# Uniform dummy matmuls, a moved output tile and a re-fitted step order in a one-core attention-then-experts kernel

## The chip, the cores and the metric

The kernel runs on one core of a Trainium2 chip. The metric is the device time of one execution in microseconds (us); lower is better. Five engines work side by side, each through its own instructions in program order: PE (matrix products, with its weight loads listed as PEld), DVE (elementwise work and reductions), ACT (activations and copies), POOL (elementwise work, masks) and SP (which issues the transfers). They wait for each other through semaphores.

## The reference

Two stages follow each other. The first is causal attention with a bias, for 8 batches of 8 heads, 576 tokens and 64 columns per head; the second is a mixture of 4 causal attention experts on the result, of which each token uses its best 2:

```python
scores = scale * np.matmul(q, k.transpose(0, 1, 3, 2))
cum = np.cumsum(np.maximum(s, 0.0), axis=-1)
bias = -(cum[:, :, :, None] - cum[:, :, None, :])
scores = np.where(causal, -1000000000.0, scores + np.minimum(bias, 0.0))
attn = softmax(scores)                       # minus the row's maximum, sum + 1e-9
x = (attn @ v), heads side by side           # 8 x 576 x 512
logits = x @ w_gate                          # the best 2 of 4 experts, their softmax weights w
for e in range(4):
    a = softmax(causal(scale * (x @ wq[e]) @ (x @ wk[e]).T))
    out += w_e * (a @ (x @ wv[e]) @ wo[e])   # 0 for tokens that did not choose e
```

## The kernel before

The work is cut into pairs: a pair is two heads (or two experts) of one batch, and there are 50 slots for them, in the order four attention pairs of a batch and then two expert pairs of the batch before. For each pair the program has some 70 small steps, each a Python function that issues a few instructions. A step is written as slot:name, and the table STEPS lists all 3508 of them in the order in which they are issued. Nothing else sets the order: every engine takes its own instructions in that order, and SP's queue of transfers likewise. The names that matter here:

- m0 to m5 (PE, L626) form rows of bf16 scores, from which M0 to M5 (DVE, L640) take the row maxima into the tile mcol. mt (PE, L660) transposes mcol, mA (ACT) copies it as mr, and mq (SP) sends it into row 96 of the query operand. The maxima of a pair are taken one or two slots before its scores.
- h, l, lq and lk split queries and keys into a high and a low half (ACT, DVE, transfers). s0 to s6 (PE, L687 and L692) are the scores from those halves, E0 to E6 (ACT) their exponentials, d0 to d3 (POOL) the masks and the sums over keys, v0 to v7 (PE, L844) the product with the values, V0 and V1 (ACT) its copy.
- a0 and a1 (PE, L894) form the sums of two pairs; r0 (SP, L922) spreads them over partitions, r1 (DVE) takes 1/x, r2 (SP, L931) writes that to DRAM, r3 and r4 (SP, L936) read it back as rows, the tile rb. n, N and o (DVE, ACT, DVE L969) scale the values with rb and split them into xh and xl.
- p (PE, L1078) are the projections of a finished batch, P (ACT) their copies, S or the last slot's z (SP) the stores; q00 to q51 (PE, L1048) and Q0 to Q5 (ACT) are the last batch's output. Of its parts, 3 and 5 are the two 256-column halves of token tile 3, and part 4 is the tile of the last 64 tokens of two batches, whose store is two transfers.
- The bank tiles in PSUM, eight of them, are taken and given back in turn, also in the order of STEPS.

Dummies are matmuls whose result is not used. The program starts with 32 of them (FIRST_IDLE), each 128 columns long with the 64-column tile of ones as weights. 48 more (IDLE) are the steps z0 to z47 of slot -2, which STEPS spreads over the first six slots: 64 columns long, with the ones as weights if the number is even and the 128-column identity if it is odd. All of them are in float32, and the trace shows two records for one.

Of the kernel before, what the change touches and what calls it, by code (L numbers as in the profile page):

```python
# [17 lines left out]
P = 128  # L18
S = 576
HS = S // 2  # L20
D = 64
# [59 lines left out]
def heads(t, at, c0, c1):  # L81
# [252 lines left out]
def tile_attention_then_moe(ctx, tc, qk, vm, vt, s, wqk, wvg, wo, out):  # L334
# [997 lines left out]
    for k in range(FIRST_IDLE):  # L1332
        idle(0, 128)
# [9 lines left out]
    def slot(n):  # L1343
# [37 lines left out]
        if n == -2 and IDLE:  # L1381
            for k in range(IDLE):
                steps[f"z{k}"] = lambda k=k: idle(k)
# [54 lines left out]
```

## Time and profile before

| | |
|---|---|
| median of 3 timed runs | 651.64 us (648.58, 651.64, 659.48) |
| the profiled execution | 647.8 us |
| its span, first to last instruction | 646.1 us |
| PE busy | 638.1 us, 99% |
| DVE, ACT, POOL busy | 548.6, 449.2, 432.1 us |
| last matmul starts | 641.40 us |

The profiled execution's own time is 1.7 us more than its span, and below all three timed runs. A matmul's end is modelled in the trace and overlaps the next one, so PE reads as busy for as long as something follows; what counts is the distance between starts. An idle time is shown in brackets, with what ended it.

### The profile page before, as it was taken

How to read it: one execution, taken by the hardware profiler on the slowest of the kernel's cores; microseconds unless marked ns; L12 is line 12 of the kernel's file. 1: busy time of each engine (PE TensorE's matmuls, PEld its weight loads, DVE VectorE, ACT ScalarE, POOL GpSimd, SP SyncE). 2: the span in 40 equal slices, each digit the busy share in tenths (PEclk: the TensorE clock that was granted, in tenths of full speed). 3: DMA queues.
4: the chain of work that ended last, by engine and by line, in shares of the span. 5: the costliest groups of instructions: out<-in, count | busy, mean ns of one | idle time of the engine just before them, and what ended most of it. 6: DMA issues, size and time to landing. Idle time of an engine off the chain costs nothing.

```text
span 646.1 us, 16548 instructions
## 1 busy us (share of the span) xinstructions
PE 638.1 (99%) x5990; PEld 542.6 (84%) x5990; DVE 548.6 (85%) x1440; ACT 449.2 (70%) x981; POOL 432.1 (67%) x530
## 2 busy tenths in 40 slices
PE   9999999999999999999999999999999999999997
PEld 8878898878888897888888888878987889789875
DVE  8989979898888977997898879898788978873984
ACT  6687777864877577776777766976685966576373
POOL 8685679786675767568766759559686777818030
PEclk9999999999999999999999999999999999999999
DMA  5355544435565376443756446465455634422323
GB/s 161 118 146 155 145 119 131 124 86 140 135 161 157 95 190 131 106 130 70 186 149 194 118 129 150 133 172 136 106 136 147 164 95 126 103 85 66 82 66 114
DMA packets 60879, 83.33 MB, mean 129 GB/s; under 512 B 26894, under 2 KB 35342, under 8 KB 60798
## 3 DMA queue, kind: packets, MB, share of 16 engines
q1 hardware_dynamic: 60798, 82.28, 49.0%
q8 instruction: 47, 0.77, 0.5%
q14 instruction: 34, 0.28, 0.2%
HBM read 44.55 MB, written 10.09 MB: 85 GB/s over the span
## 4 chain that ended last, share of the span: by engine, by line
PE 89%; DVE 6%; DMA 2%; ACT 2%; issue 1%; SPq 0%; DVEq 0%; ACTq 0%
PE pvp L844 18%; PE pq L1078 15%; PE s L687 11%; PE s L692 10%; PE mx L626 9%; PE pw L1078 7%; PE po L1078 7%; PE sm L894 3%; DVE mx L640 3%; PE idle L1326 3%; DMA rb<-rr 2%; PE po L1048 1%; PE mt L660 1%; PE gt L1205 1%; DVE mcol L640 1%
## 5 line engine op out<-in xcount | busy, mean ns | idle before, releaser
L640 DVE CUSTOM_DVE_ANT_0 mx<-mx,mask 128x256 f32<-128x256 f32 (+7 forms) x432 | 194.2, 468 | 34.9 <-PE mx L626 19.1
L708 ACT ACTIVATE p<-s 128x512 f32<-128x512 f32 x288 | 161.4, 588 | 60.4 <-PE s L692 55.1
L726 POOL TENSOR_SCALAR_AFFINE_SELECT p<-p 128x256 f32<-128x256 f32 (+2 forms) x183 | 113.5, 621 | 105.9 <-ACT p L708 97.9
L687 PE MATMUL s<-q,k 128*128 128x288 f32 (+5 forms) x672 | 169.1, 285 | 1.0 <-DVE q L600 0.7
L692 PE MATMUL s<-q,k 97*128 97x288 f32 (+5 forms) x672 | 160.8, 279 | 0.0
L687 PEld LDWEIGHTS s<-q,k 128*128 128x128 f32 (+1 forms) x672 | 122.5, 182 | 10.0 <-issue 3.3
L773 POOL TENSOR_TENSOR r<-r,p 128x640 f32<-128x640 f32 x84 | 119.4, 1421 | 6.8
L692 PEld LDWEIGHTS s<-q,k 97*128 97x128 f32 (+1 forms) x672 | 121.6, 182 | 1.1
L600 DVE TENSOR_TENSOR q<-raw,q 64x576 fp32r<-64x576 f32 (+1 forms) x86 | 86.0, 1008 | 19.5 <-ACT q L560 14.5
L844 PE MATMUL pvp<-p,v 128*64 128x320 f32 (+6 forms) x1024 | 95.6, 334 | 0.4 <-DVE mcol L640 0.4
L844 PEld LDWEIGHTS pvp<-p,v 128*64 128x64 f32 x1024 | 66.5, 137 | 26.2 <-issue 1.1
L605 DVE TENSOR_TENSOR k<-raw,k 64x576 fp32r<-64x576 f32 (+1 forms) x86 | 84.6, 991 | 2.6 <-DMA k<-k 0.2
L626 PE MATMUL mx<-k,q 96*64 96x256 bf16 (+7 forms) x960 | 79.1, 293 | 0.1
L1078 PE MATMUL pq<-xh,wqkh 128*128 128x288 f32 x256 | 76.4, 298 | 0.0
L1078 PE MATMUL pq<-xl,wqkh 128*128 128x288 f32 x256 | 75.5, 295 | 0.6 <-DVE xl L969 0.6
L1078 PE MATMUL pq<-xh,wqkl 128*128 128x288 f32 x256 | 75.4, 294 | 0.0
L563 ACT ACTIVATE k<-raw 64x576 fp32r<-64x576 f32 x96 | 64.6, 680 | 2.4 <-DMA raw<-in_qk_dram 0.6
L560 ACT ACTIVATE q<-raw 64x576 fp32r<-64x576 f32 x96 | 64.1, 679 | 2.9 <-DVE mcol L640 1.7
L640 DVE DVE_READ_ACCUMULATOR2_ANT mcol<- 128x1 f32 x480 | 65.3, 136 | 0.8
L626 PEld LDWEIGHTS <-q 96*64 96x64 bf16 x960 | 46.5, 109 | 21.4 <-issue 7.0
L858 ACT ACTIVATE pv<-pvp 128x320 f32<-128x320 f32 (+1 forms) x92 | 35.9, 403 | 33.4 <-PE pvp L844 33.3
L767 POOL TENSOR_TENSOR r<-p 128x128 f32<-128x128 f32 x37 | 22.2, 599 | 49.5 <-ACT p L708 49.5
(157 smaller groups left out, 1224.3 us busy)
## 6 DMA issues: line engine op xcount, KB each, us to landing
raw<-in_qk_dram SPq DMA_DIRECT2D x30, 576.0 KB
rb<-rr SPq DMA_DIRECT2D x92, 144.0 KB
q<-q SPq DMA_DIRECT2D x45, 288.0 KB
k<-k SPq DMA_DIRECT2D x39, 288.0 KB
v<-in_vm_dram SPq DMA_DIRECT2D x32, 256.0 KB
out_dram<-o SPq DMA_DIRECT2D x31, 256.0 KB
q<-mr SPq DMA_DIRECT2D x96, 2.2 KB
out_dram<-o SPq DMA_DIRECT2D x10, 128.0 KB
```

The lines of the kernel that those rows point to most:

```text
L563: nc.scalar.activation(k2[0:64, j], get_raw(n, j)[64:128], AF.Copy)
L600: eng.tensor_tensor(a[64:128, j], get_raw(n, j)[0:64], q2[0:64, j].bitcast(F32), op=OP.subtract)
L605: eng.tensor_tensor(c[0:64, j], get_raw(n, j)[64:128], c[64:128, j].bitcast(F32), op=OP.subtract)
L626: nc.tensor.matmul(t[64 * j : 64 * j + 64, c0 : c0 + k1 - k0], q2[0:RC, 64 * qt : 64 * qt + 64], k2[0:RC, k0:k1], start=True, stop=True,)
L640: nc.vector.tensor_tensor_reduce(t[:, c0 : c0 + w], t[:, c0 : c0 + w], mask[:, m0 : m0 + w], scale=1.0, scalar=mcol[n][:, 9:10] if slot == ...
L687: nc.tensor.matmul(t[0:nk, c0 : c0 + q1 - q0], K1[r1(n)][:, j, k0 : k0 + nk], Q1[r1(n)][:, j, q0:q1], start=True, stop=False,)
L692: nc.tensor.matmul(t[0:nk, c0 : c0 + q1 - q0], K2[r2(n)][0 : RM + 1, j, k0 : k0 + nk], Q2[r2(n)][0 : RM + 1, j, q0:q1], start=False, stop= ...
L708: nc.scalar.activation(chunk_of(ci, 0, 512)[:, x % 2], tl[x], AF.Exp, scale=0.125)
L726: nc.gpsimd.affine_select(out=a, in_=a, pattern=[[0, a.shape[1]], [1, w]], compare_op=OP.is_ge, fill=0.0, base=0, channel_multiplier=-1,)
L773: add(r[:, :, q0:S], r[:, :, q0:S], chunk_of(2, c, c + S - q0), op=OP.add)
L844: nc.tensor.matmul(cur[h][64 * j : 64 * j + 64, q0 - PVC[h] : q1 - PVC[h]], vsl(j, kt), heads(ptile[n], at, c, c + q1 - q0)[:, j], start=f ...
L1078: nc.tensor.matmul(t[0:nk, 0:w], l, r, start=(x == 0), stop=(x == len(terms) - 1))
```

## The change

The dummies become one kind: 128 columns long, with the 64 ones as weights, all 80 of them. At the end, the 64-token tile (q40, q41, Q4, z4) goes ahead of the second halves (q30 to Q3, q50 to Q5), and the store of the first half (z3) goes behind its later part. And the table STEPS lists the same 3508 steps in another order in some stretches: from the 620th entry to the 869th (slots 7 to 11), from the 1495th to about the 1886th (slots 20 to 26, with small moves up to slot 29), from the 2495th to the 2869th (slots 33 to 39) and from the 3120th to the 3369th (slots 42 to 49). No step is added or left out, and the table's first 619 entries stay.

```diff
-    "8:h3 7:P1 8:s5 8:s4 7:e0 8:s1 8:E1 8:n0 8:g0 8:g1 8:s3 8:g2 8:n1 8:E3 8:s2 8:E2 8:s0 8:mt 8:mA "
+    "8:h3 7:P1 8:s5 8:s4 7:e0 8:s1 8:E1 8:n0 8:g0 8:g1 8:s3 8:g2 8:n1 8:E3 8:s2 8:E2 8:s0 7:d3 8:mt "
...
-    "49:yo2 49:q30 49:Q2 49:q31 49:Q3 49:q40 49:z1 49:z2 49:q41 49:Q4 49:z3 49:q50 49:z4 49:q51 49:Q5 "
+    "49:yo2 49:q40 49:Q2 49:q41 49:z1 49:Q4 49:z2 49:q30 49:q31 49:z4 49:Q3 49:q50 49:q51 49:z3 49:Q5 "
     "49:z5"
 )
...
-    def idle(k, cols=64):
+    def idle():
         if not idle_bank:
             idle_bank.append(take("idle"))
-        w, m = (ident, P) if k % 2 else (ones, D)
         nc.tensor.matmul(
-            idle_bank[0][0:m, 0:cols], w, ones[:, 0:1].to_broadcast([P, cols]),
+            idle_bank[0][0:D, 0:P], ones, ones[:, 0:1].to_broadcast([P, P]),
             start=True, stop=True,
         )
...
     for k in range(FIRST_IDLE):
-        idle(0, 128)
+        idle()
...
         if n == -2 and IDLE:
             for k in range(IDLE):
-                steps[f"z{k}"] = lambda k=k: idle(k)
+                steps[f"z{k}"] = idle
```

PE at the start of the program, one piece of the difference (p_75 is the tile that holds the ones, p_74 the one that holds the identity; rows of one kind in a row are counted with an x):

```order
-L1326 MATMUL idle<-p_75 64x128 x32
-L1326 MATMUL idle<-p_75 64x64
-L1326 MATMUL idle<-p_75,p_74 128x64
...
+L1325 MATMUL idle<-p_75 64x128 x40
 L626 LDWEIGHTS q_0_68
 L626 MATMUL mx_0_190<-k_0_71,q_0_68 64x448
```

The first eight step dummies, which alternated, now continue the 32 of the start; the next group, after the first six rows of maxima, becomes 14 of the same kind.

SP in slots 8 to 10, around the sums of batch 1's last two pairs (sr, rr and rb are their way through DRAM, r0, r2 and r3/r4), before:

```order
L922 DMA sr_1760<-rs_1747 128x1x18
L551 DMA k_2_73<-cum 3x2x576
L669 DMA q_0_68<-mr_1726 1x9x64 x2
L931 DMA rr_1855<-sr_1760 128x18
L593 DMA k_0_66<-k_1_72 64x1152
L521 DMA v_106<-in_vm_dram 128x2x256
L522 DMA v_106<-in_vt_dram 64x2x64
L582 DMA q_0_64<-q_1_69 64x1152
L936 DMA rb_1_1917<-rr_1855 64x576 x2
L936 DMA rb_0_1970<-rr_1855 64x576 x2
```

and with the change:

```order
L582 DMA q_0_64<-q_1_69 64x1152
L551 DMA k_2_73<-cum 3x2x576
L669 DMA q_0_68<-mr_1733 1x9x64 x2
L922 DMA sr_1826<-rs_1747 128x1x18
L931 DMA rr_1835<-sr_1826 128x18
L593 DMA k_0_66<-k_1_72 64x1152
L936 DMA rb_1_1874<-rr_1835 64x576 x2
L936 DMA rb_0_1895<-rr_1835 64x576 x2
```

Between rr and rb three transfers less are issued: the values of the next pair (L521, L522) and a copy of queries (L582).

DVE ahead of the transpose of pair 38's maxima (mx38_2 is the bank of M2, mx38_4 that of M4; ISA rows with two operands are the reductions), before:

```order
L640 ISA mx38_0_7145,mcol38_7125<-mx38_0_7145,mask_86 128x64
...
L605 TENSOR_TENSOR k1_0_66<-raw2_5_0_6652,k1_0_66 64x576
L600 TENSOR_TENSOR q1_1_65<-raw2_5_2_6843,q2_0_68 64x576
...
L969 TENSOR_TENSOR yl_103<-pv33_6545,yh_102 128x512
L969 TENSOR_TENSOR zl_105<-pv33_6545,zh_104 128x64
L640 ISA mx38_2_7083,mcol38_7125<-mx38_2_7083,mask_86 128x320
...
L640 ISA mx38_2_7083,mcol38_7125<-mx38_2_7083,mask_86 128x192
```

and with the change:

```order
L640 ISA mx38_2_7113,mcol38_7106<-mx38_2_7113,mask_86 128x192
...
L600 TENSOR_TENSOR q1_0_64<-raw2_5_0_6652,q2_2_70 64x576 x2
L640 ISA mx38_5_7101,mcol38_7106<-mx38_5_7101,mask_86 128x256
...
L640 ISA mx38_4_7151,mcol38_7106<-mx38_4_7151,mask_86,mcol38_7106 128x320
...
L969 TENSOR_TENSOR yl_103<-pv32_6580,yh_102 128x512
```

The accumulator reads and repeated rows between them are left out. The last reduction of the pair is now the one of bank 4, with the reduction of bank 5 right before it; on PE, three score chunks, one group of 12 projections and the small chunk s6 stand between that bank's matmuls and the transpose.

## Rows read from the trace of the kernel before

**Rows 1.** The page: busy time by engine, and the granted clock of PE in 40 slices, in tenths of its full speed.

```profile
PE 638.1 (99%) x5990; PEld 542.6 (84%) x5990; DVE 548.6 (85%) x1440; ACT 449.2 (70%) x981; POOL 432.1 (67%) x530
...
PEclk9999999999999999999999999999999999999999
```

**Rows 2.** PE's waits over the whole span, without the one at its very start: engine, line, releaser, us in total, times, longest.

```profile
PE s L687 <- DVE q L600: 0.7, 1, 0.7
PE pq L1078 <- DVE xl L969: 0.6, 1, 0.6
PE pvp L844 <- DVE mcol L640: 0.4, 1, 0.4
PE mt L660 <- DVE mcol L640: 0.3, 1, 0.3
```

**Rows 3.** Busy time in stretches between chosen times: length, then PE, PEld, DVE, ACT, POOL busy, granted clock, DMA share and GB/s.

```profile
105.00:150.00 45.00, 43.42 (x436) 36.23 (x435) 41.89 (x116) 33.21 (x72) 35.51 (x39) 1.00 0.45 121
...
255.00:330.00 75.00, 75.00 (x709) 63.30 (x704) 65.92 (x179) 54.35 (x119) 52.58 (x64) 1.00 0.47 120
...
430.00:505.00 75.00, 75.00 (x709) 64.25 (x708) 63.63 (x171) 52.68 (x116) 58.05 (x69) 1.00 0.55 136
```

**Rows 4.** PE in order of time at the start, each row from a narrow window: start, us, what, number of records.

```profile
1.05 4.74 PE L1326 MATMUL idle<-p 128*64 128x128 f32 x21 [1.05 <-DVE p L358]
...
6.00 4.38 PE L1326 MATMUL idle<-p 128*64 128x128 f32 x38
...
12.52 0.43 PE L1326 MATMUL idle<-p,p 128*128 128x64 f32 x2
12.88 1.48 PE L626 MATMUL mx<-k,q 96*64 96x448 bf16 x20
14.19 0.28 PE L1326 MATMUL idle<-p 128*64 128x64 f32 x2
...
18.50 0.88 PE L626 MATMUL mx<-k,q 96*64 96x512 bf16 x10
```

**Rows 5.** Weight loads of the dummies, by shape: line, engine, operation, shapes, count, busy us, mean ns.

```profile
L1326 PEld LDWEIGHTS idle<-p 128*64 128x64 f32 x112 | 14.6, 155 | 3.0 <-DVE p L358 1.1
L1326 PEld LDWEIGHTS idle<-p,p 128*128 128x128 f32 x48 | 7.2, 188 | 1.8 <-issue 0.4
```

**Rows 6.** DVE in order of time at the start.

```profile
13.46 0.63 DVE L640 CUSTOM_DVE_ANT_0 mx<-mx,mask 128x448 f32<-128x448 f32 x1 [1.04 <-POOL k L352]
...
18.51 0.14 DVE L640 DVE_READ_ACCUMULATOR2_ANT mcol<- 128x1 f32 x1
19.20 0.50 DVE L640 CUSTOM_DVE_ANT_0 mx<-mx,mask 128x320 f32<-128x320 f32 x1 [0.54 <-PE mx L626]
```

**Rows 7.** Stretches of the start, columns as in rows 3.

```profile
20.00:30.00 10.00, 10.00 (x92) 8.95 (x88) 9.55 (x39) 7.36 (x16) 4.35 (x7) 1.00 0.37 110
30.00:40.00 10.00, 9.44 (x108) 7.53 (x107) 9.80 (x23) 9.67 (x20) 9.74 (x23) 1.00 0.36 117
```

**Rows 8.** PE in order of time: the three long waits between 130 and 150 us.

```profile
133.20 0.39 PE L687 MATMUL s<-q,k 128*128 128x320 f32 x1 [0.65 <-DVE q L600]
...
137.38 0.40 PE L1078 MATMUL pq<-xl,wqkh 128*128 128x288 f32 x1 [0.60 <-DVE xl L969]
...
149.80 0.28 PE L660 MATMUL mt<-p,mcol 128*9 128x128 f32 x1 [0.33 <-DVE mcol L640]
```

**Rows 9.** The chain that ended last, in order of time, from 122 us on: start, us, what.

```profile
123.75 0.76 SPq L522
...
125.25 0.55 SPq L936
...
125.85 4.73 DMA rb<-rr
...
130.70 0.55 DVE pv L961
...
134.30 3.03 DVE xl L969 x2
...
137.38 3.71 PE pq L1078 x26
```

**Rows 10.** SP in order of time: the transfer that writes 1/x to DRAM.

```profile
121.99 0.36 SPq L931 DMA_DIRECT2D rr<-sr  x1
```

**Rows 11.** PE and DVE in order of time around the transpose of pair 38: the last matmuls of its maxima, the DVE's first reduction after them, its last accumulator read, and the transpose.

```profile
475.51 0.63 PE L626 MATMUL mx<-k,q 96*64 96x256 bf16 x8
...
476.06 0.43 DVE L640 CUSTOM_DVE_ANT_0 mx<-mx,mask 128x256 f32<-128x256 f32 x1 [1.51 <-PE mx L626]
...
483.15 0.14 DVE L640 DVE_READ_ACCUMULATOR2_ANT mcol<- 128x1 f32 x1
...
483.75 0.27 PE L660 MATMUL mt<-p,mcol 128*9 128x128 f32 x1
```

**Rows 12.** The end: the last matmul, ACT's copies and SP's stores in order of time.

```profile
641.40 0.28 PE L1048 MATMUL po<-woh,xl 128*128 128x256 f32 x1
...
641.05 1.04 ACT L1055 ACTIVATE o<-po 128x512 f32<-128x512 f32 x2 [1.05 <-PE po L1048]
...
641.68 1.12 SPq L1035 DMA_DIRECT2D out_dram<-o  x2
642.89 0.54 SPq L1064 DMA_DIRECT2D out_dram<-o  x1
```

352 rows, old and new, of the table STEPS are left out of this document.

## The prediction

> **What bounds the kernel now.** I read the page first: PE is busy for 638.1 of 646.1 us, and its granted clock stands at full in all 40 slices [rows 1]. Since a matmul's drawn end runs into the next one, that share proves little; so next the view of PE's waits. It holds four waits behind the start, 2.0 us together [rows 2]. The view by stretches says where: between 105 and 150 us PE misses 1.58 us of 45, but from 255 to 330 us and from 430 to 505 us nothing at all, while DVE stands idle 9 and 11 us there [rows 3]. So the kernel is a row of matmuls without holes in most places, and the reader is to see two things: an order that moves no matmul out and none in can only give back waits that exist, and in stretches without any it can only make new ones. The start is another matter: there dummies fill PE [rows 4], and DVE does the work, 9.55 and 9.80 us of 10 [rows 7].
>
> **The dummies.** The old step dummies cost 0.31 us each: 14 of them lie between 14.19 and 18.50 us [rows 4]. The new kind has run already, as the first 32: at full pace 38 records take 4.38 us [rows 4], 0.11 us from start to start without the last one's overhang, two records for a dummy, so 0.22 us. (At the very start 21 records take 4.74 us, half that pace, at a granted clock that reads full; those dummies are unchanged.) So the new ones are twice as long in columns and still shorter in time, because they never change the weights. The group of eight ahead of 12.88 us gives back 8 x 0.09 = 0.7 us and the one of 14 1.2 us; I take off 0.1 us for each group, whose last dummy still meets new weights. The other 26 stand in 14 groups of one to four: 26 x 0.09 - 14 x 0.1 = 0.9 us. Together about 2.6 us of PE's time, at most.
>
> A rule speaks against this. By the row, a load of the 64 ones takes 0.155 us on average [rows 5], longer than the 0.11 us between two starts, so it lies beside the matmul before it. The Trainium skill (TensorE: Matmul & The Clock Gate, The mechanism) says that a weight load overlaps matmuls in flight only when it is for another group of rows, and these dummies all use all rows. By that rule a dummy would cost the more the more loads it has, and the sum would rise where mine falls; the trace does not agree for this kind. It is the fourth rival below.
>
> What of it is on the path? DVE's first reduction waits 1.04 us and starts at 13.46 [rows 6]; the view names a POOL memset of another buffer, but the first row of maxima comes off PE then. Eight shorter dummies bring it 0.6 us forward. The six banks then keep DVE busy until 18.65, where it waits 0.54 us for PE, which has 14 dummies in the way [rows 4, 6]. With 1.1 us fewer of them plus the 0.6 us, PE is there at 16.8 and DVE does not wait. From 19.2 us on DVE is all but full, so what counts is DVE's gain: 0.6 + 0.54 = 1.1 us. The rest becomes waits of PE. Later groups add 0.1 us where DVE has air. **-1.2 us**; bounds 0 (DVE waits for POOL after all, and something else holds it at 19.2) and -2.6.
>
> **The order, 105 to 150 us.** Three waits: scores for DVE's low half of the queries 0.65, a projection for xl 0.60, the transpose for mcol 0.33 [rows 8], together 1.58 us. Projections start every 3.71 / 26 = 0.14 us [rows 9] but are drawn some 0.3 to 0.4 us long [rows 8], so a wait is up to 0.17 us longer than shown: at most 2.1 us. The chain tells why: SP, which issued rr at 121.99 [rows 10], comes to rb at 125.25 only, behind the value loads (the second ends at 124.51) and a query copy; rb needs 4.73 us to land; only then does DVE scale (130.70) and, being in order, make the scores' low half; its two xl then take 3.03 us and PE has them at 137.38 [rows 9]. The change issues rb straight after one key copy, without the two loads and the query copy between. With 0.36 us for rr and 0.5 to 0.6 for the copy, rb goes out near 123.0, some 2 us earlier, more than both waits. The transpose at 149.80 belongs to pair 12: by the order it now has five score chunks more of PE work behind its last maxima, 0.5 us each (four records at the pace of a projection or less). What is late next is the split behind rb (N, o), which stands right ahead of the projection in the new order as in the old; I leave 0.2 us of wait there. The transfers that are passed: the loads of values come later, but they are needed a slot later; they cost nothing while that slot lasts, and at most one load's 3 us if it does not. **-1.4 us**; bounds 0 and -2.1.
>
> **The order, from 255 us.** No wait to remove [rows 3]; 0 at best. The likely price is at transposes. Pair 38 is the plainest: its last maxima leave PE at 476.1, DVE works without a stop from 476.06 to 483.29, and the transpose follows at 483.75, 0.46 us later [rows 11]. Now only three score chunks, s6 and a projection group stand between, 3 x 0.5 + 0.3 + 12 x 0.14 = 3.5 us in place of 7.7. DVE's own work there shrinks too, from 7.2 us to the reductions of banks 5 and 4 (1.6 us at the pace of before, four instructions of 0.4 to 0.6 us), as the order shows. If DVE comes to them on time, no wait; I put down **+0.6 us** for this one and others like it, bounds 0 and +6 (second rival).
>
> **The end.** PE ends with the same matmul at the same distance. The last copy is done at 642.09, but its store goes out at 642.89, since SP is still issuing the 64-token tile's two transfers (1.12 us from 641.68 on) [rows 12]. In the new order these two start after Q4, 0.7 us earlier as one more half tile of PE work stands behind it, and one store of 0.35 us comes between. The last store goes out about 0.4 us earlier. **-0.3 us**; bounds 0 and -0.8.
>
> **Sum.** -1.2 - 1.4 + 0.6 - 0.3 = -2.3 us, made against the profiled execution's 647.8: 645.5 us. The timed runs lie above it, by 0.8 us (lowest) and 3.8 us (median). I take the lower end, the pace without disturbance, a little raised: **646.5 us**.
>
> **Rivals.**
> 1. *The start is DVE's, and nothing else gains.* DVE at 9.8 of 10 speaks for it [rows 7]; its wait of 0.54 us for PE speaks against. Then the start gives 0.2, the rest as above without the 105 us stretch, which may find a new wait for each old one: 647.8 - 0.2 + 0.6 - 0.3 = 647.9, timed about 648.7. 20%.
> 2. *Transposes wait for DVE: slower than before.* In the new order four pairs (24, 26, 38, 49) have their transpose closer behind their last maxima. Priced as if DVE were as far behind as it was: pair 38 waits 7.7 - 3.5 - 0.46 = 3.7 us, and the other three I put at half as much together, 1.9 us. It decides once these waits pass 2.9 us, the sum of the gains. For it: DVE's unbroken 7.2 us [rows 11], and the wait at 149.80 [rows 8]. Against: DVE has 11 us idle in that stretch [rows 3] and its order was moved along. 647.8 - 2.9 + 5.6 = 650.5, timed 651.3. 17%.
> 3. *All of it.* Both bounds: 647.8 - 2.6 - 2.1 - 0.8 = 642.3, timed 643.1. 8%.
> 4. *The new dummies cost more*, if a load cannot lie beside a matmul once other work is mixed in: 0.155 + 0.11 per record, 0.53 a dummy, 48 x 0.22 = 10.6 us more, of which what is not on the path is PE's fill; at most 647.8 + 10.6 - 1.7 = 656.7. The rows of 32 in a line speak against it. 2%. That is also the case in which the change does not do what it says.
>
> The forecast has 53%.
>
> **Numbers.** The range reaches from the third rival to just past the second: 643 to 652 us. A measurement of this kernel can tell 2%, 13 us, from no change; no case but the fourth comes near it, and what is left for the outer chances is mostly the runs' own scatter (1.7% between the three): faster 0.03, within 0.94, slower 0.03.
>
> **What would show it.** In the profile after: dummies at 0.11 us a record in every group; DVE's first reduction near 12.9 and no wait at 18.1; PE's waits between 105 and 150 us down from 1.58 to about 0.2 us; rb on the chain no more; the last store some 0.4 us closer behind the last matmul. Wrong would be: a wait of PE for mcol of over 1 us at one of the four transposes, PE idle in 255 to 330 or 430 to 505 us, or a second round of DVE reductions that still starts past 18.9 us (19.20 now).

## The result and the profile after

The changed kernel takes 656.23 us (median of 13 runs, 654.32 to 661.21); the kernel before, run beside it, 653.1 us (13 runs, 648.3 to 659.48). The ratio is 1.0085, 95% interval 1.0058 to 1.0112: a little slower, with 1 outside the interval, and by less than the 2% that the prediction takes as the least that such a measurement tells. The ratio compares fast runs alone, without those that lie more than 1.5% above their kernel's fastest, so it need not be the quotient of the two medians. The forecast was 646.5 us, a gain, with a range of 643 to 652; the time is a loss and lies above the range. The profiled execution took 658.38 us, span 656.7, which is 10.6 us more than the span of before.

The stretches that the prediction looked at come first, columns as in [rows 3]:

```profile
20.00:30.00 10.00, 9.92 (x87) 8.71 (x83) 9.55 (x35) 7.84 (x16) 5.56 (x8) 1.00 0.50 154
...
105.00:150.00 45.00, 45.00 (x447) 38.61 (x444) 39.95 (x116) 33.90 (x75) 33.61 (x38) 1.00 0.53 139
255.00:330.00 75.00, 72.61 (x662) 60.63 (x663) 64.32 (x180) 50.70 (x111) 47.87 (x57) 1.00 0.45 119
430.00:505.00 75.00, 68.41 (x640) 56.66 (x640) 56.17 (x146) 47.80 (x104) 52.24 (x66) 0.95 0.45 116
505.00:545.00 40.00, 40.00 (x367) 32.97 (x364) 32.43 (x92) 28.02 (x61) 25.86 (x30) 0.97 0.45 119
```

From 105 to 150 us PE has no hole left. From 255 to 330 us it misses 2.4 us and from 430 to 505 us 6.6 us, where it missed nothing before, and the granted clock, which stood at 1.00 throughout, reads 0.95 and 0.97 behind. PE's waits answer to [rows 2]:

```profile
PE sm L894 <- POOL r L778: 6.9, 2, 6.6
PE pw L1133 <- DVE mcol L640: 1.5, 1, 1.5
...
PE mx L626 <- ACT p L708: 0.7, 1, 0.7
PE s L687 <- DVE mcol L640: 0.7, 3, 0.3
PE mt L660 <- DVE mcol L640: 0.7, 2, 0.5
```

One wait is longer than the others together: the sums of pairs 36 and 37 (steps a1 and a0 of slot 38, line L894) wait 6.6 us for POOL. PE around it, in order of time:

```profile
494.06 0.68 PE L894 MATMUL sm<-r,p 128*32 128x288 f32 x4
501.33 2.13 PE L894 MATMUL sm<-r,p 128*32 128x288 f32 x12 [6.59 <-POOL r L778]
```

Then the question is what POOL was doing. In the kernel before, its first and last rows of d0 to d3 of pair 37 were these, and the sums started at 494.62 us without a wait:

```profile
481.88 0.41 POOL L726 TENSOR_SCALAR_AFFINE_SELECT p<-p 128x256 f32<-128x256 f32 x1 [1.20 <-ACT p L708]
...
489.71 0.47 POOL L778 TENSOR_TENSOR r<-r,p 128x128 f32<-128x128 f32 x1
```

The same rows with the change, with the last row of pair 36 ahead:

```profile
475.13 0.46 POOL L778 TENSOR_TENSOR r<-r,p 128x128 f32<-128x128 f32 x1
492.09 0.41 POOL L726 TENSOR_SCALAR_AFFINE_SELECT p<-p 128x256 f32<-128x256 f32 x1 [16.50 <-DVE g L1166]
...
500.82 0.45 POOL L778 TENSOR_TENSOR r<-r,p 128x128 f32<-128x128 f32 x1
```

POOL stood idle for 16.5 us and then needed 9.2 us (8.3 before). What ended its idle time is the rank of the gates (step g2 of slot 38), on DVE:

```profile
490.88 0.42 DVE L1147 TENSOR_TENSOR vx<-pw,vx 64x260 f32<-64x260 f32 x1 [2.08 <-ACT vx L1144]
...
491.68 0.24 DVE L1165 TENSOR_TENSOR g<-g,p 128x80 f32<-128x80 f32 x1
491.84 0.24 DVE L1166 TENSOR_TENSOR g<-g,tgt 128x80 f32<-128x80 f32 x1
```

Masking scores and ranking experts share no data. They share a tile: the rank's first mask, tlt (line 392), lies in spare columns of the tile p that odd pairs use, L1165 reads it there, and d0's columns of the two heads lie on both sides of the spare ones. Whoever comes second in the table waits for the first. In the old table d0 of pair 37 stood at entry 2710 and g2 at 2747; in the new one g2 stands at 2734 and d0 at 2739. The instruction lists say it in one row, before and after:

```
418 L726 AFFINE_SELECT p_75<-p_75 128x2x128 [waits PE_49,Activation_49]
418 L726 AFFINE_SELECT p_75<-p_75 128x2x128 [waits DVE_49,PE_49,Activation_49]
```

The program ranks eight times, and in the trace this rank alone holds POOL up. So POOL got DVE to wait for, DVE waited for the last projection of the gates' logits (L1147), and the sums waited for POOL. The clock followed, in stretches of 5 us:

```profile
490.00:495.00 5.00, 4.74 (x35) 3.84 (x33) 3.94 (x10) 4.17 (x10) 2.74 (x5) 1.00 1.01 319
495.00:500.00 5.00, 0.00 (x0) 0.00 (x0) 1.21 (x2) 1.00 (x3) 4.84 (x5) 0.74 0.14 49
500.00:505.00 5.00, 3.67 (x22) 1.59 (x24) 0.76 (x3) 1.44 (x3) 4.66 (x11) 0.50 0.02 5
505.00:510.00 5.00, 5.00 (x45) 3.59 (x42) 3.07 (x12) 2.06 (x5) 4.47 (x4) 0.74 0.44 113
```

With 1.00 for 2.4 GHz and 0.50 for 1.2, the three lower stretches lose 5 x (0.26 + 0.50 + 0.26) = 5.1 us of clock, some 10 us at the lower level, of which the part up to 501.3 us lies in the wait and costs nothing.

What did go as forecast, at the start and at the end, in rows of DVE, PE, PE, ACT and SP ([rows 4, 6, 12]):

```profile
12.97 0.63 DVE L640 CUSTOM_DVE_ANT_0 mx<-mx,mask 128x448 f32<-128x448 f32 x1 [0.64 <-PE mx L626]
13.66 2.94 PE L1325 MATMUL idle<-p 128*64 128x128 f32 x25
...
652.20 0.28 PE L1048 MATMUL po<-woh,xl 128*128 128x256 f32 x1
652.52 0.38 ACT L1055 ACTIVATE o<-po 128x256 f32<-128x256 f32 x1 [0.33 <-PE po L1048]
652.97 1.03 SPq L1064 DMA_DIRECT2D out_dram<-o  x2
```

To see where every kernel below gains and loses, I cut each trace at the same four pieces of work, the 8th, 19th, 35th and 43rd of ACT's copies of the transposed maxima (mA, L664). In the kernel before they start at 93.66, 228.47, 432.55 and 532.33 us, in the changed one at 91.87, 224.49, 431.99 and 542.27. The changed order of slots 7 to 11 lies between the first two, that of slots 20 to 29 between the second and third, that of 33 to 39 between the third and fourth. Differences to the kernel before, in us, of profiled executions:

| kernel | to 1st mark (start) | to 2nd (slots 7-11) | to 3rd (20-29) | to 4th (33-39) | to the last matmul (42-49) | tail | span |
|---|---|---|---|---|---|---|---|
| changed | -1.79 | -2.19 | +3.43 | +10.50 | +0.85 | -0.22 | +10.58 |
| 1 rank behind d3 | -1.69 | -2.21 | +0.62 | +0.60 | +0.86 | -0.24 | -2.07 |
| 2 mask in its own tile | -1.38 | -2.16 | +1.90 | +0.25 | +0.85 | -0.23 | -0.77 |
| 3 before, d0-d2 late | +3.94 | +0.02 | -0.69 | +8.61 | +0.52 | +0.01 | +12.41 |
| 4 dummies alone | -1.37 | -0.05 | +3.64 | -0.02 | +0.09 | 0.00 | +2.29 |
| 5 own tile, old dummies | -0.45 | -2.12 | +2.47 | +0.25 | +0.83 | -0.22 | +0.76 |
| 6 wait filled | -1.28 | -2.19 | +2.65 | +8.14 | +1.09 | -0.22 | +8.20 |
| 7 own tile, 20-39 as before | -1.12 | -2.16 | +0.14 | +0.01 | +0.86 | -0.23 | -2.49 |
| 8 own tile, order as before | -2.13 | +0.06 | +4.38 | -0.01 | +0.71 | -0.01 | +2.99 |
| 9 dummies, 7-11, end | -1.52 | -2.19 | +3.34 | -0.03 | -0.11 | -0.25 | -0.76 |
| 10 the same and 20-29 | -1.52 | -2.20 | +0.78 | -0.03 | +0.05 | -0.24 | -3.16 |

Most of the changed kernel's loss is in one column. How far executions of the same code differ shows in the first column: up to that mark all these kernels have the same order, and the nine with the new dummies still lie between -1.12 and -2.13, experiment 5 with the old ones at -0.45.

The profiled execution of before, at 647.8 us, was also one of its better ones. Each timed run has a mean granted clock. 10 us at the lower level take 5.1 / 650 = 0.008 from it, so a mean near 0.992 tells of such a spell. The timed runs, counted by that mean (medians in brackets; experiments 3 and 6, which change the place of the wait itself, are left out):

| runs | 0.993 or less | 0.994 to 0.997 | 0.998 and more |
|---|---|---|---|
| before, 77 beside the experiments | 17 (653.8 us) | 23 (653.2) | 37 (648.8) |
| changed, 13 | 3 (656.2) | 10 (656.0) | 0 |
| experiment 5: old dummies, changed order, 12 | 4 (654.3) | 3 (653.5) | 5 (650.1) |
| experiments 4, 7, 8, 9: new dummies, 20-29 as before, 44 | 0 | 13 | 31 |
| experiments 1, 2, 10: new dummies, 20-29 changed, 30 | 0 | 1 | 29 |

Read so, the kernel before loses the clock somewhere in 40 of 77 runs, the changed one in all 13. Where in a timed run it was lost the mean does not tell.

### The profile page after: what moved, and what is told of

Read it like the earlier page. It is cut to its first block, busy times and chain, and to the rows that moved or that the text cites. A ratio compares the mean times of both kernels' runs of the same rounds, so it can differ in the third digit from the quotient of the medians.

```text
span 656.7 us, 16556 instructions
## 1 busy us (share of the span) xinstructions
PE 640.2 (97%) x5990; PEld 542.9 (83%) x5990; DVE 551.3 (84%) x1440; ACT 449.9 (69%) x981; POOL 434.1 (66%) x530
## 4 chain that ended last, share of the span: by engine, by line
PE 85%; DVE 5%; DMA 3%; POOL 2%; issue 1%; SPq 1%; ACT 1%; DVEq 0%; POOLq 0%
PE pvp L844 17%; PE pq L1078 15%; PE s L687 11%; PE s L692 10%; PE mx L626 9%; PE pw L1078 6%; PE po L1078 6%; PE sm L894 3%; DVE mx L640 3%; PE idle L1325 2%; DMA rb<-rr 1%; DMA k<-k 1%; PE po L1048 1%; POOL r L773 1%; PE gt L1205 1%
## 5 line engine op out<-in xcount | busy, mean ns | idle before, releaser
L726 POOL TENSOR_SCALAR_AFFINE_SELECT p<-p 128x256 f32<-128x256 f32 (+2 forms) x183 | 111.1, 608 | 128.5 <-ACT p L708 90.9
L600 DVE TENSOR_TENSOR q<-raw,q 64x576 fp32r<-64x576 f32 (+1 forms) x86 | 88.4, 1040 | 18.0 <-ACT q L560 13.3
L844 PE MATMUL pvp<-p,v 128*64 128x256 f32 (+6 forms) x1024 | 97.9, 338 | 0.3 <-DVE mcol L640 0.3
L605 DVE TENSOR_TENSOR k<-raw,k 64x576 fp32r<-64x576 f32 (+1 forms) x86 | 85.1, 997 | 14.0 <-DMA k<-k 12.1
L844 PEld LDWEIGHTS pvp<-p,v 128*64 128x64 f32 x1024 | 68.0, 139 | 27.0 <-issue 1.9
L626 PE MATMUL mx<-k,q 96*64 96x256 bf16 (+7 forms) x960 | 81.3, 293 | 0.8 <-ACT p L708 0.7
L626 PEld LDWEIGHTS <-q 96*64 96x64 bf16 x960 | 48.2, 109 | 22.4 <-issue 7.9
L1078 PEld LDWEIGHTS pq<-xh,wqkh 128*128 128x128 f32 x256 | 48.2, 188 | 0.6 <-issue 0.4
```

The source lines that it names most:

```text
L600: eng.tensor_tensor(a[64:128, j], get_raw(n, j)[0:64], q2[0:64, j].bitcast(F32), op=OP.subtract)
L605: eng.tensor_tensor(c[0:64, j], get_raw(n, j)[64:128], c[64:128, j].bitcast(F32), op=OP.subtract)
L626: nc.tensor.matmul(t[64 * j : 64 * j + 64, c0 : c0 + k1 - k0], q2[0:RC, 64 * qt : 64 * qt + 64], k2[0:RC, k0:k1], start=True, stop=True,)
L726: nc.gpsimd.affine_select(out=a, in_=a, pattern=[[0, a.shape[1]], [1, w]], compare_op=OP.is_ge, fill=0.0, base=0, channel_multiplier=-1,)
L844: nc.tensor.matmul(cur[h][64 * j : 64 * j + 64, q0 - PVC[h] : q1 - PVC[h]], vsl(j, kt), heads(ptile[n], at, c, c + q1 - q0)[:, j], start=f ...
L1078: nc.tensor.matmul(t[0:nk, 0:w], l, r, start=(x == 0), stop=(x == len(terms) - 1))
```

## The experiments

**Theory A** is the one above: the shared tile makes POOL wait for the rank, PE waits for POOL, the clock falls with PE idle. The rival **B**: the POOL steps themselves are late, since they stand later in the table (d0 from entry 2710 to 2739). In the experiments the line numbers are up to three lower or six higher. They ran on three chips, each with the kernel before beside them: 1 to 4 on one, 5 to 8 on a second, 9 and 10 on a third. So medians compare well within such a group, and ratios across them.

**1. The rank behind the POOL steps.** One step of the changed table moves:

```diff
-38:S0 38:g2 38:n1
+38:S0 38:n1
...
-38:l1 37:d3 38:a1
+38:l1 37:d3 38:g2 38:a1
```

> The changed kernel with one step moved: the gates' rank of slot 38 (g2, DVE) goes from ahead of the sums of pair 37 on POOL (d0 to d3) to directly behind them. Theory A, POOL's d0 of pair 37 waits for the rank, because the rank reads its tie mask from spare columns of the tile p that d0 writes: POOL starts d0 by 486 us in place of 492.1, PE's wait at the sums of slot 38 falls from 6.6 us to between 0 and 1, and since PE no longer stands idle the granted clock stays at full speed there; the profiled execution is about 6.6 + 5 us shorter, near 647, and the median some 6 to 11 us below the changed kernel's 656.2, so 645 to 650, about that of the kernel before or 3 us under it. Rival B, POOL is late because d1 to d3 themselves stand 35 entries later in the table: the wait at the sums stays above 5 us and the time within 1 us of the changed kernel's.

Measured: 648.42 us (12 runs, 645.74 to 650.35), ratio to the kernel before 0.9955 [0.9924, 0.9986], clock 0.999 or 1.000 in every run. POOL's first and last rows of pair 37:

```profile
480.77 0.41 POOL L724 TENSOR_SCALAR_AFFINE_SELECT p<-p 128x256 f32<-128x256 f32 x1 [7.92 <-ACT p L706]
...
488.12 0.46 POOL L776 TENSOR_TENSOR r<-r,p 128x128 f32<-128x128 f32 x1
```

POOL now waits for ACT's exponentials and starts 11.3 us earlier (2.7 of them because the whole program is that much earlier at the third mark), the long wait at the sums is gone, and so is the fall of the clock. B falls: d0 to d3 stand where they stood.

**2. The same order, the mask elsewhere.** Only the place of the data changes:

```diff
-    tlt = PB[1][:, PSPARE + D + 5 * E : PSPARE + P - 4].bitcast(BF16)
-    tlt = tlt.rearrange("p (t a b) -> p t a b", a=E, b=E)
+    tlt = const.tile([P, 1, E, E], BF16, tag="tlt", name="tlt")
...
-            nc.vector.tensor_tensor(g1, g1, tlt, op=OP.mult)
+            nc.vector.tensor_tensor(g1, g1, tlt.to_broadcast([P, 5, E, E]), op=OP.mult)
```

> The changed kernel with its whole order kept; only the tie mask that the rank reads lies in a tile of its own (one copy of 16 columns, read for all five token tiles) and no longer in spare columns of the tile p. Theory A: POOL's d0 of pair 37 has no wait for DVE left, PE's wait at the sums of slot 38 falls from 6.6 us to between 0 and 1 and the clock stays at full speed; profiled execution near 647, median 645 to 650. Rival B, the order of the POOL steps itself is late: 6.6 us stay. What both leave: the 1.5 us wait at 256 us, which this edit does not touch.

Measured: 646.07 us (7 runs), ratio 0.991 [0.9875, 0.9945]. POOL's d0 of pair 37:

```profile
482.41 0.41 POOL L725 TENSOR_SCALAR_AFFINE_SELECT p<-p 128x256 f32<-128x256 f32 x1 [7.92 <-ACT p L707]
```

With the order untouched the wait for DVE is gone. So it was the tile together with the order, not the order by itself. A wait at 256 us stays, 0.8 us here.

**3. The kernel before made to wait.** Its d0 to d2 of pair 37 go behind the rank:

```diff
-37:d0
...
-37:d1 37:d2
...
-38:g2
+38:g2 37:d0 37:d1 37:d2
```

> The kernel before with three steps moved: d0, d1 and d2 of pair 37 (POOL) go from 33 to 37 entries ahead of the rank of slot 38 to directly behind it. Theory A: POOL waits for the rank, which DVE finished at 492.4 us in the kernel before, then needs 8.3 us for d0 to d3 as before, and PE, which began the sums at 494.6, waits about 6 us for them; the granted clock then falls to half for some 10 us, about 5 us more: the time is 8 to 12 us above the kernel before in the profile, ratio 1.009 to 1.018. Rival B, only the order within POOL counts and its steps have 5 us of slack: PE waits less than 1 us and the ratio is within 0.997 to 1.004. Rival C, the wait comes but the clock does not fall: ratio 1.007 to 1.010.

Measured: 659.3 us (6 runs), ratio 1.0111 [1.0066, 1.0157]. POOL's d0 and the two waits of PE at the sums:

```profile
495.71 0.41 POOL L724 TENSOR_SCALAR_AFFINE_SELECT p<-p 128x256 f32<-128x256 f32 x1 [11.75 <-DVE g L1164]
```

```profile
503.23 1.19 PE L892 MATMUL sm<-r,p 128*32 128x288 f32 x8 [4.68 <-POOL r L771]
505.08 1.18 PE L892 MATMUL sm<-r,p 128*32 128x288 f32 x4 [0.66 <-POOL r L776]
```

The expected 6 us of wait are 5.3, the granted clock falls behind them (0.73 from 500 to 505 us, 0.58 from 505 to 510), and the stretch loses 8.6 us: the wait can be made as well as taken away, and rival C, no fall of the clock, is out. But this trace holds a second thing that nobody moved: it loses 3.9 us ahead of the first mark. The start, columns as in [rows 7]:

```profile
10.00:20.00 10.00, 10.00 (x79) 7.33 (x80) 8.13 (x27) 5.13 (x9) 9.70 (x8) 0.88 0.34 80
20.00:30.00 10.00, 10.00 (x66) 8.35 (x63) 5.88 (x26) 4.66 (x11) 1.35 (x2) 0.61 0.20 60
```

With the old dummies and PE drawn as busy throughout, the clock lost 10 x (0.12 + 0.39) = 5.1 us in 10 to 30 us, where the profile of before shows 1.00.

**4. The dummies alone.**

```diff
-    def idle(k, cols=64):
+    def idle():
...
-        w, m = (ident, P) if k % 2 else (ones, D)
...
-            idle_bank[0][0:m, 0:cols], w, ones[:, 0:1].to_broadcast([P, cols]),
+            idle_bank[0][0:D, 0:P], ones, ones[:, 0:1].to_broadcast([P, P]),
```

> The kernel before with the new dummies alone (128 columns, 64 ones as weights), its order kept. By the trace of the changed kernel the start is 1.45 us shorter by the scores at 47.6 us, and nothing after it depends on the dummies: scores that began at 49.07 us begin near 47.6, and the time is 1 to 1.6 us below the kernel before, ratio 0.9975 to 0.9985. Rival: a transfer or a wait later in the program gives the gain back by 150 us: ratio 0.999 to 1.001.

Measured: 648.65 us (12 runs), ratio 0.9949 [0.9912, 0.9986]. The trace gains 1.4 us up to the first mark, as expected; the median gains 2.8, more than expected. The difference fits the second table: runs at 0.993 and less, 17 of 77 before, are none of 12. The profiled run itself was worse than that of before, through a wait at 271 us, in the old order of slots 20 to 29:

```profile
269.13 0.42 PE L624 MATMUL mx<-k,q 96*64 96x448 bf16 x4 [0.41 <-ACT p L706]
271.40 0.34 PE L685 MATMUL s<-q,k 128*128 128x224 f32 x1 [1.85 <-issue]
```

```profile
270.00:275.00 5.00, 3.47 (x16) 2.97 (x17) 4.86 (x21) 1.47 (x4) 4.75 (x6) 0.81 0.16 51
275.00:280.00 5.00, 5.00 (x24) 3.99 (x22) 3.30 (x10) 2.99 (x7) 2.76 (x7) 0.85 0.48 174
```

After 1.85 us of waiting the clock lost another 5 x (0.19 + 0.15) = 1.7 us. The profile names no releaser ("issue"), but the scores start 0.1 us behind the end of a row of DVE's maxima (it ends at 271.30 us). The same wait in experiments 8 and 9 (1.86 us each) ends 0.1 us behind the same row of DVE too (271.68 and 270.06 us). So it is most likely a wait for DVE; no run removes it to show this.

**5. The changed order with the old dummies**: the edit of 4 undone in the kernel of 2.

```diff
-    def idle():
+    def idle(k, cols=64):
...
+        w, m = (ident, P) if k % 2 else (ones, D)
...
-            idle_bank[0][0:D, 0:P], ones, ones[:, 0:1].to_broadcast([P, P]),
+            idle_bank[0][0:m, 0:cols], w, ones[:, 0:1].to_broadcast([P, cols]),
```

> The changed order and the mask in its own tile, as in the run with that edit (median 646.07 us), but with the dummies of the kernel before: two kinds, 64 columns, ones and identity in turn. Theory A, the old dummies cost 1.45 us in every run and, in some runs, the clock as well: the run of the kernel before with d0 to d2 moved showed half clock from 17.65 to 27.89 us, and 9 of 24 timed runs of the kernel before have a mean granted clock of 0.993 or less, against none of the 12 with the new dummies alone. So several runs here come back to a clock near 0.992 at 651 to 653 us, the others lie near 647.5, and the median is 647.5 to 651. Rival B, the old dummies cost their 1.45 us and nothing else: no run below 0.996, median 647 to 648.

Measured: 652.11 us (12 runs, 647.4 to 657.4), ratio 1.001 [0.9976, 1.0044]. The mean clocks of 0.991 to 0.992 are back in 4 of 12 runs, as theory A has it; the median is 1 us above what it gave. (The expectation counts 9 of 24 runs of before at 0.993 or less; they are 8.) So the old dummies cost 0.9 us at the start in the trace (-0.45 against -1.38, a difference as large as that between executions with one kind) and the clock in a third of the runs. That is not all: the five runs at a full clock lie at 647.4 to 651.5 us, median 650.1, where A had 647.5. The rest stays unexplained.

**6. The late sums kept late, the wait filled with matmuls.**

```diff
             t[h] = take(f"sm{n}_{h}")
+            if n == 37 and h == 1:
+                for _ in range(28):
+                    nc.tensor.matmul(
+                        t[h][0:64, 0:128], WOH[:, 0, 0:64].bitcast(F32),
+                        WOH[:, 0, 0:128].bitcast(F32), start=True, stop=True,
+                    )
```

> The changed kernel with the late sums of slot 38 kept late, but 28 matmuls whose result is overwritten (64-column weights, 128 columns, float32, 2 records each) put on PE directly ahead of them: 28 x 0.22 us = 6.2 us of work in the place of the 6.6 us wait. Theory A, the granted clock fell because PE stood idle: PE's wait there falls below 1 us with POOL's sums as late as before, the clock stays at full speed, and the median is 3 to 5 us below the changed kernel's 656.2, 651 to 653. Rival B, the clock's fall costs little or has another cause: the clock still falls near 497 us, or the time stays within 1.5 us of 656.2.

Measured: 655.62 us (12 runs), ratio 1.0067 [1.0038, 1.0097], profiled 656.04. PE at the place, and the clock there:

```profile
493.83 6.33 PE L893 MATMUL sm<-woh 128*64 128x128 f32 x56
...
501.12 1.17 PE L900 MATMUL sm<-r,p 128*32 128x288 f32 x12 [0.35 <-POOL r L778]
```

```profile
495.00:500.00 5.00, 5.00 (x48) 4.91 (x46) 0.98 (x2) 0.77 (x2) 4.84 (x5) 1.00 0.12 42
500.00:505.00 5.00, 4.65 (x54) 2.67 (x54) 2.03 (x7) 1.77 (x4) 4.74 (x10) 1.00 0.03 8
```

A is right about the cause, since with PE busy the clock stays at full: it is 0.997 to 1.000 in all 12 runs, against 0.990 to 0.995 in the 13 of the changed kernel. It is wrong about the size. Slots 33 to 39 lose 8.14 us instead of 10.50, so the fall of the clock was worth 2.4 us in the profiled execution, not 5; and the ratios, 1.0067 and 1.0085, have intervals that overlap. The time, within 1.5 us of the changed kernel's, is the one that rival B gave. The lateness of the sums is nearly the whole price.

**7. New order only in slots 7 to 11, 42 to 49 and at the end** (mask in its own tile): the entries of STEPS for slots 20 to 29 and 33 to 39 as before. Their beginnings, against the kernel of 2:

```diff
-20:n0 20:V1 21:m3 21:lk 21:r0 21:hc 20:M2 21:m4
+20:n0 20:g1 21:m3 21:r0 21:m4 20:M2 20:M1 21:h2
...
-34:l3 34:E5 35:M5 33:d3 34:mq 35:h1 34:v5 34:v6
+34:l3 34:mq 35:M3 34:M1 34:v5 35:lk 33:d3 35:l2
...
```

> Mask in its own tile, new dummies, the changed order in slots 7 to 11 and 42 to 49 and at the end, but the order of the kernel before in slots 20 to 29 and 33 to 39. Theory A, the re-fitted order of these slots is worth nothing once POOL no longer waits for the rank: median within 1 us of the run with the changed order throughout (646.07), 645 to 647.1. Rival B, that order gains something there which the late sums hid: 647.5 to 650. Rival C, it costs through the waits at 255 to 275 us (2.9 us in the trace of the changed kernel): 643 to 645.

Measured: 645.06 us (8 runs), ratio 0.9926 [0.9886, 0.9967]: 1 us from the 646.07 of experiment 2, the limit that A had set, and 0.06 us from the 645 of C. The five runs at a full clock have a median of 644.5 us, the six of experiment 2 one of 646.0, but on another chip, and by the ratios (0.9926 and 0.991) nothing is gained. The old order loses the clock in 3 of 8 runs. A and C are not told apart here.

**8. The old order with the mask in its own tile** and the new dummies: experiment 4 with the edit of 2.

```diff
-    tlt = PB[1][:, PSPARE + D + 5 * E : PSPARE + P - 4].bitcast(BF16)
...
+    tlt = const.tile([P, 1, E, E], BF16, tag="tlt", name="tlt")
...
```

> The order of the kernel before with the new dummies and the mask in its own tile. In that order no step of POOL stood waiting for the rank. Theory A: the tile of its own is worth nothing there, and the time is that of the new dummies alone, 648.65 within 1.5 us, ratio to the kernel before 0.993 to 0.998. Rival B, other steps of POOL that write to the tile p wait for the rank there too (or DVE's reads of the mask wait for POOL): 646 to 647, ratio below 0.9925.

Measured: 646.71 us (12 runs), ratio 0.9959 [0.9926, 0.9993]; experiment 4, with the mask where it was, had 0.9949. By the ratios, which share out the differences between chips, the tile of its own gains nothing in the old order. Its median is 1.9 us lower than that of 4, past the 1.5 that A allowed, but that of the kernel before beside it is lower by 1.4 as well (650.03 against 651.42), and 4 had five runs with a lower clock and 8 two. That is not settled to the microsecond.

**9 and 10. What is worth keeping.** STEPS as before, but for slots 7 to 11 and the end (9), and slots 20 to 29 as well (10); the new dummies in both; the mask where it was. Against experiment 4, the beginning of the first stretch, the end, and for 10 the beginning of the third piece:

```diff
-8:s0 8:mt 8:mA 8:E0 7:d3 8:s6 8:hc 8:a0
+8:s0 7:d3 8:mt 8:s6 8:mA 8:hc 8:a1 8:a0
...
-49:q30 49:Q2 49:q31 49:Q3 49:q40 49:z1 49:z2 49:q41 49:Q4 49:z3 49:q50 49:z4 49:q51 49:Q5
+49:q40 49:Q2 49:q41 49:z1 49:Q4 49:z2 49:q30 49:q31 49:z4 49:Q3 49:q50 49:q51 49:z3 49:Q5
...
-20:n0 20:g1 21:m3 21:r0 21:m4 20:M2 20:M1 21:h2
+20:n0 20:V1 21:m3 21:lk 21:r0 21:hc 20:M2 21:m4
...
```

> The kernel before with three parts of the change: the new dummies, the changed order in slots 7 to 11, and the 64-token tile ahead of the last halves. Slots 20 to 29, 33 to 39 and 42 to 49 keep their order. Theory A, the parts add up as the traces so far have them: 1.4 us at the start, 2.2 in slots 7 to 11 and 0.2 at the end, 3.8 together, and no loss after 430 us (in four traces the new order of slots 42 to 49 cost 0.8 us there): runs at a full clock lie between 642.5 and 645, the profiled one near 644; some runs still show a clock of 0.995 to 0.997 and 647 to 650 us, as the order of slots 20 to 29 before does; median 643.5 to 646, ratio 0.989 to 0.993. Rival B, the gains are given back at the next wait for a transfer, at 250 to 275 us: median 646 to 649.

> The same with the changed order of slots 20 to 29 as well. Theory A, that order trades runs that lose the clock near 272 us for waits of PE at 256 to 275 us that cost 0.7 to 3.5 us in every run: no run below a clock of 0.996, full-clock runs 1 to 2.5 us above those without it, median within 1 us of the other's. Rival B, it only costs: median 1.5 us or more above the other's. Rival C, it only gains: median 1.5 us or more below it.

Measured: 645.96 us (12 runs), ratio 0.9915 [0.9884, 0.9946], for 9, and 646.07 us (11 runs, 644.4 to 647.72), ratio 0.991 [0.9877, 0.9943], for 10. Both beat both kernels, by about 1%. For 9 the parts add up at the first two marks and at the end (-1.52, -2.19, -0.25), and nothing is lost after 430 us, as A has it; but its profiled execution, 647.05 us in place of 644, gave 3.34 us back in slots 20 to 29, as rival B has it, and the median lies on the border between the two. 9 has three runs at 0.995 to 0.997 and full-clock runs from 642.5 to 647.2, median 644.8; 10 has none below 0.998 and the smaller scatter, and their median, 646.07, is 1.2 us higher. That is what A says of 10, but such a cost is still within the scatter of the runs. The clock is the better shown half: with the new dummies 13 of 44 runs lose it in the old order of slots 20 to 29, and 1 of 30 in the new one. The waits are not the new order's alone: between 255 and 276 us each of its six traces has waits of PE of 0.6 to 2.9 us in sum, but of the six with the old order three have none (before, 3 and 7) and three have 2.4 to 3.2 us (4, 8 and 9). In the trace of 10 that stretch lost 0.6 us of PE:

```profile
255.00:330.00 75.00, 74.37 (x692) 62.10 (x692) 63.64 (x171) 52.69 (x116) 48.58 (x61) 1.00 0.48 125
```

## Why the prediction was wrong

- **The start, forecast -1.2: -1.8 in the changed kernel's trace, -1.1 to -2.1 in the eight others with the new dummies.** Right within what executions differ, and by the steps given: a dummy record takes 0.11 us in its groups, DVE's first reduction starts at 12.97 (forecast 12.9) and waits for PE, not for POOL, and the wait at 19.20 [rows 6] is gone. The first rival (the start gains 0.2) and the fourth (loads that cannot lie beside a matmul) both fall. That the fourth's 656.7 us is close to the measured 656.23 is luck: it made the dummies dearer, and they became cheaper. What was missed is the second effect: the old dummies cost the clock in some runs, which the one trace of before could not show.
- **105 to 150 us, forecast -1.4: -2.1 to -2.2 in all eight traces with that order.** Right in mechanism, too small: none of the three waits is left, where I kept 0.2 us of one. rb is issued at 121.71 us, 1.2 us behind the end of rr, with only the key copy between, and PE's wait for xl does not come back. The upper bound of 2.1 was the size to take.
- **The order from 255 us, forecast +0.6, bounds 0 and +6: +14.8 in the profiled execution (3.43 + 10.50 + 0.85).** This is the step that failed. It asked at which transpose PE would wait for DVE, and from 255 us on no transpose waits, that of pair 38 included (the two in the list of PE's waits stand at 18 and 59 us). Most of the price, the 10.50, came by POOL, whose queue the step did not follow, through a tile whose two users have nothing to do with each other. The evidence was there to read: in the list of instructions, row 418 had gained a wait for DVE, and the table had moved g2 across d0. It also left out that a long wait of PE can take the clock with it, 2.4 us here. The list of signs did name the place (PE idle in 430 to 505 us would be wrong); the second rival had the sign and the stretch, and the wrong wait in it. In the timed runs the shared tile is worth some 8 to 10 us: 656.23 us fall to 648.42 and 646.07 in experiments 1 and 2.
- **The rest of that step.** Slots 33 to 39 without the late sums: +0.25 to +0.6 in three traces. Slots 42 to 49: +0.8 to +1.1 in the six traces with the new order and -0.1 to +0.7 with the old; 0.29 us of it is a wait of sums for POOL at 576 us, the rest is not explained. Slots 20 to 29: +0.6 to +3.4 with the new order (six traces), and -0.7 to +0.1 or +3.3 to +4.4 with the old (five). There DVE's wait for a copy of keys (L605), 3.8 us in the changed kernel, is 4.0 in experiment 8, 4.1 in 9 and 2.6 in 4 with the old order, 0.2 in 3 and 7, and none in the profile of before. So it is not the new order's alone, though all six traces of that order have it (0.8 to 4.3 us); what the order adds to it stays open.
- **The end, forecast -0.3: -0.22 to -0.25 in all eight traces with it.** Right.
- **The level.** The sum stood on one execution of 647.8 us, and I took "the pace without disturbance, a little raised". In 77 later runs the kernel before had that pace in 37; in the others the clock fell. A forecast for the median had to start from 651 to 653. That would have put it at about 650 and would not have saved it: the failing term is larger. (A 9 in [rows 1] means 90% or more, not full: in that trace the clock is 0.90 from 640 to 645 us and 0.50 behind. The last matmul starts at 641.40, so little hung on it.)

## What to carry to other kernels

When a step moves, look not only at who needs its result but at every tile that it touches, spare columns included: compare, instruction by instruction, which engines each one waits for before and after, and price a row that gains one. Data that shares a tile with other work only to save space ties two engines' orders together; 32 bytes per partition of its own removed the tie here. And when timed runs scatter by 1.7% and all lie above the one profile, count how often each loses the clock before trusting a sum made on that profile.

## What the hardware showed that was not expected

The granted clock fell in a stretch in which PE was not seen waiting: in experiment 3, with the old dummies, 0.88 and 0.61 between 10 and 30 us at a busy share of 10.00 of 10. The Trainium skill (TensorE: Matmul & The Clock Gate, Why this matters for your kernels) puts drops of throughput in the middle of a kernel down to PE standing idle between bursts. The wait of 6.59 us in the changed kernel, behind which the clock was 0.50, agrees with that, and experiment 6, in which the same 6 us were filled and the clock stayed at 1.00, agrees again; the start of experiment 3 does not. Whether it was the alternating weights or the fewer columns of the old dummies was not tried; with the new ones the fall near 0.992 came in none of 74 runs that had no late sums.

At one place of the program a wait of 1.85 us was followed by a lower clock in experiment 4 (0.81 and 0.85) and one of 1.86 us in experiment 8 (0.88 and 0.78), while one of 1.86 us in experiment 9 was not (1.00 and 1.00).
